# Seven products instead of eight for a third of the later gate and value projections

## The chip, the core and the metric

The kernel runs on one NeuronCore of a Trainium2 chip. The metric is the device time of one execution, in microseconds (us); a time of several runs is their median. The core has five engines that work side by side, each through its own instructions in the order in which they were written: TensorE (PE in the profile; PEld is its loading of weights), VectorE (DVE), ScalarE (ACT), GpSimd (POOL) and SyncE (SP, which here only starts transfers). Matrix products are written into PSUM, which has eight banks of 128 partitions by 512 float32.

## The reference: what is computed

Inputs are q, k, v of shape (4 batches, 8 heads, 768 tokens, 64), 16 centroids for each head, and the weights of a gated feed-forward layer, `w_gate` and `w_val` (512 x 1536) and `w_out` (1536 x 512). The part before the feed-forward layer is attention within clusters:

```
q_assign = argmax(normalised q . normalised centroids)   # k_assign the same way
scores   = (q . k) / 8, or -1e9 where q_assign != k_assign
attn     = softmax(scores) . v
x        = attn with the heads side by side: 3072 tokens x 512
```

The part that the change is about:

```
gate = 1 / (1 + exp(-(x @ w_gate)))
val  = x @ w_val
out  = (gate * val) @ w_out
```

## The kernel before

**Types and layout.** Products take float16 operands and sum in float32, except the turning of inputs (a product with an identity) and the products with centroids, which take float32. Batches are `b` = 0..3; each has two token groups, `gr` = 0 and 1. Both groups of a later batch have 384 tokens; in batch 0 they have 256 and 512. So there are eight groups. Heads go in pairs, four pairs to a batch.

**Attention.** For each group and pair of heads, PE makes scores (L986), ACT their exponentials from one of two score buffers of two banks each (`sc`, L1010), PE multiplies these with the values (L1037) into one bank (`av`), and DVE divides by the sums (L1062, L1067). The result `xn` is turned by a DMA of the SP queue (L1095), seldom by PE (L1075), into `x`, four chunks of 128 features by the group's tokens. The inputs of the next batch are brought in meanwhile: loads into `nat` buffers, DVE transposes (L573), POOL casts (L628, and L499 for the values), products with centroids (L665), a few DVE steps that make the cluster rows, and DMAs that place them.

**Feed-forward layer.** `feed` (L1359) makes the 12 feature chunks of one group. `proj` (L1365) is the product of one chunk: four PE instructions (L1372) that take the four chunks of `x` against a 128 x 128 block of weights each, with the group's tokens as columns (384 for most), into one of three `ring` banks. A chunk needs two of them, one for the gate and one for the value. ACT makes the tanh of the gate's bank into a `gt` buffer (L1390), and DVE multiplies it with the value's bank into `hT` (L1401). `project` (L1165) then makes the output rows of two blocks of 128 tokens at a time. It does so already by seven products for eight (Strassen's scheme in Winograd's form): five sums of `hT` parts on DVE (L1221), seven products of six instructions of 256 columns (L1252) in two banks, and ACT, DVE and POOL steps that add up between the products (L1277 to L1325). `sum_weights` (L1127) makes the sums of `w_out` once.

**What sets the order.** No instruction is placed by hand. `Order` (from L39) is a planner that runs when the kernel is built. Every step is a task with an engine, an assumed duration, the tasks that it depends on, a due time and the buffers that it takes or uses. `schedule` goes through time, and at each step gives the engine that is free first the task that can start first (within 0.02 us: the one that is due first). The order in which tasks are chosen is the order in which they are emitted, for each engine. A task that takes a buffer must get one of the tag's slots: `free_slots` (L70) gives the slots of a tag in turn, so a task waits for the slot whose turn it is. Tags can inherit slots of another tag (`HEIRS`): the buffers named `late` (loads of later batches, and spare room in the last `project`) are slots of `nat` that are no longer needed.

Of the kernel before, what the change touches and what calls it, by code (L numbers as in the profile page):

```python
# [9 lines left out]
FP = mybir.dt.float32  # L10
# [28 lines left out]
class Order:  # L39
# [6 lines left out]
    ANY = ()  # L46
# [154 lines left out]
def kernel(  # L201
# [32 lines left out]
        "nat": 9, "t32": 4, "even": 6, "odd": 6, "oht": 3, "t1": 2, "mx": 2, "ohf": 2,  # L234
# [13 lines left out]
        "gt": ([128, 512], FP), "out2": ([128, 2, DM], FP),  # L248
# [35 lines left out]
    NVP = 6  # L284
# [21 lines left out]
    S1, T1 = 96, 52.6  # L306

    def due_at(slot):
        return T1 + (slot - S1) * (0.414 if slot < S1 else 0.826)

    def due_ffn(work):
        return 36.0 + work * 1.82
# [93 lines left out]
    c4 = od.add("DVE", 1.65, c_scale, [c1], due=-8.8, seq=[c2])  # L406
# [85 lines left out]
    def load_v(b, p, eng, due, due_cast, early=0.0, behind=()):  # L492
# [5 lines left out]
                "POOL", 0.5,  # L498
# [58 lines left out]
    def prepare(b, grp, due, step, act=(), queues=("SP",), split=False):  # L557
# [5 lines left out]
        for p, nm in sides:  # L563
            t32[p, nm] = Buf("t32")
            for half in range(2):
                if quarters(b, p):

                    def turn_blocks(p=p, nm=nm, half=half):
# [10 lines left out]
                        "DVE", 0.55, turn_blocks, nat[b, p, nm], due, lat=0.15,  # L579
# [20 lines left out]
                def copy(p=p, nm=nm, half=half, rb_=rb_):  # L600
# [11 lines left out]
                    "ACT" if (nm, half) in act else "DVE", 0.5, copy,  # L612
                    [tr], due, lat=0.15, uses=[rb_, t32[p, nm]],
# [4 lines left out]
        for p in grp:  # L618
            ev, od_ = aug[b, p] = Buf("even"), Buf("odd")
            prev = []  # L620
            for half in (0, 1) if split else (None,):
# [13 lines left out]
                for nm in ("k", "q"):  # L635
# [3 lines left out]
                            "POOL", 0.83 * part, lambda nm=nm, cast=cast: cast(nm),  # L639
# [34 lines left out]
        for half in range(2):  # L674
# [10 lines left out]
            def back(cols=cols, oh=oh, half=half):  # L685
# [4 lines left out]
                "DVE", 0.53,  # L690
                lambda t1=t1, half=half: turn_scores(take(t1)[:n], rg.tile[:n, half, :QB]),
                [cl], due, acq=[t1], uses=[rg],
            )
            a2 = od.add(
                "DVE", 0.52,
                lambda t1=t1, mx=mx: top_scores(take(mx)[:n], t1.tile[:n]),
                [a1], due, acq=[mx], uses=[t1], lat=0.0,
            )
            a3 = od.add("DVE", 0.55, same, [a2], due, acq=[oh], uses=[t1, mx], lat=0.0)
            if quarters(b, grp[0]):  # L700
                a3 = od.add("DVE", 0.25, weigh, [a3, c_small], due, uses=[oh], lat=0.0)
            a5 = od.add(
                "DVE", 0.38, back, [a3], due, seq=turned[-1:],
# [4 lines left out]
            if split or half:  # L708
                n_ = 0
                cs = cols if split else ALL  # L710
                for e in range(2):
                    for pos, p in enumerate(grp):
                        for g, nm in ((2 * pos, "k"), (2 * pos + 1, "q")):
# [7 lines left out]
                                [a5, shifted[b, p, half]], due - (20.0 if (b, grp[0]) == (1, 0) else 0),  # L721
                                uses=[oht, aug[b, p][e]], lat=1.5,
# [5 lines left out]
    def place(b, p, ohf, tiles, last, due, alloc, c):  # L728
# [6 lines left out]
        for n_, (e, nm, h) in enumerate(rows):  # L735
            g = tiles.index((nm, h))
            m = od.add(
                "DVE", 0.395,
# [4 lines left out]
                [last, *alloc], due + 0.3 * n_ + (0.0 if n_ > 5 else 0.0), uses=[ohf, aug[b, p][e]],  # L743
# [13 lines left out]
    def prepare_pair(b, p, due, step, act=("q",), direct=False):  # L757
# [3 lines left out]
        for h in range(2):  # L761
            for nm in ("k", "q"):
# [15 lines left out]
                def copy(nm=nm, cols=cols, rg=rg):  # L778
# [12 lines left out]
                    "ACT" if nm in act else "DVE", 0.5, copy, [tr], due, lat=0.15, uses=[rg, t32[nm]]  # L791
# [4 lines left out]
        for nm, e in (("k", 0), ("q", 0), ("k", 1), ("q", 1)):  # L796
            to = od_ if e else ev

            def cast(nm=nm, e=e, to=to):
# [4 lines left out]
                "POOL", 0.83, cast, [cp[nm, 0], cp[nm, 1]], due + 0.1 * e,  # L804
# [27 lines left out]
        for dur, go, acq, uses in (  # L832
            (0.61, lambda: turn_scores(take(t1), rg.tile[:, :QB]), t1, [rg]),
            (0.55, lambda: top_scores(take(mx), t1.tile), mx, [t1]),
            (0.67, same, oh, [t1, mx]),
            (0.55, lambda: turn_matches(take(oht)[:, :QB], oh.tile), oht, [oh]),
        )[: 3 if direct else 4]:
            last = od.add("DVE", dur, go, [last], due, lat=0.0, acq=[acq], uses=uses)
# [24 lines left out]
    def prepare_first(due):  # L863
# [8 lines left out]
        for nm, h in (("k", 0), ("k", 1), ("q", 0), ("q", 1)):  # L872
# [34 lines left out]
            cp[nm, h] = od.add(on, 0.5, copy, [tr], due, lat=0.1, uses=[rg, t32[nm]])  # L907
# [30 lines left out]
        for dur, go, acq, uses in (  # L938
            (0.58, lambda: turn_scores(take(t1), rg.tile[:, :QB]), t1, [rg]),
            (  # L940
                0.55,
# [19 lines left out]
    def attend(block, at, slot):  # L961
# [13 lines left out]
        early = slot < 108.0  # L975
        t1 = []
        for i, (e, j) in enumerate(some):
            kb = aug[b, p][j % 2]

            def score(i=i, e=e, j=j, kb=kb):  # L980
# [16 lines left out]
                    due - (32.5 if early else 0.0), lat=0.25,  # L997
# [6 lines left out]
        def exponentials():  # L1004
# [16 lines left out]
            "ACT", 0.13 + 0.00078 * together * N, exponentials,  # L1021
            [*t1, c_small, c3], due, lat=0.2, acq=[es], uses=[sc],
# [8 lines left out]
        def value():  # L1031
# [15 lines left out]
            due + (-4.1 if last else 3.5) - (23.5 if early else 0.0), lat=0.25 if last else 0.0,  # L1047
# [52 lines left out]
        t4 = od.add("DVE", 0.17 + 0.02 * nq, rec, [t3], due - 18.0, lat=0.05, acq=[rr], uses=[av])  # L1100
        t5 = od.add("DVE", 0.14 + 0.15 * nq, norm, [t4], due - 18.0, lat=0.2, acq=[xn], uses=[av, rr])
        if not ((b, gr) == (0, 0) and p >= 2 or (b, p) == (0, NP - 1) or block == blocks[-1]):
# [11 lines left out]
                "DVE", 0.1 + 0.133 * nq, out_of_bank, [t6], due - 18.0, lat=0.2, seq=xd[:1],  # L1114
# [12 lines left out]
    def sum_weights(due):  # L1127
# [26 lines left out]
        for kind, dur in (("1112", 0.84), ("2122", 0.84), ("1122", 0.42)):  # L1154
# [10 lines left out]
    def project(b, one, two, final, many, end):  # L1165
# [45 lines left out]
        def add(to, place, x, y, op, behind=()):  # L1211
            tasks = []
            for n, (i0, i1) in enumerate(parts):
# [4 lines left out]
                        "DVE", 0.15 + 0.067 * (i1 - i0),  # L1218
                        first(
                            fresh,  # L1220
                            lambda i0=i0, i1=i1: nc.vector.tensor_tensor(  # L1221
# [4 lines left out]
                        due - -10.0 - (6.0 if end and not n else 0.0), lat=0.15, acq=fresh,  # L1226
# [11 lines left out]
        a6 = add([], lambda: a(1, 0), lambda: a(1, 0), lambda: a(0, 0), ALU.subtract, a22)  # L1238
        a7 = add([], lambda: a(0, 1), lambda: a(0, 1), lambda: a(1, 1), ALU.subtract, a12)
# [3 lines left out]
        def product(ring, bank, new, lo, hi, left_, right, deps, acq, uses, n0=0, runs=((0, NFC // 2),)):  # L1243
# [33 lines left out]
            "ACT", 0.4, first(fresh_hf, lambda: nc.scalar.mul(t_hf(), t_r1()[:, HM:], 0.5)), [m2], due, lat=0.2,  # L1277
# [4 lines left out]
            "DVE", 0.42,  # L1282
# [4 lines left out]
            "DVE", 0.42, lambda: stt(t_hf(), t_r2()[:, HM:], 0.5, t_df()[:, 1], ALU.mult, ALU.add),  # L1287
# [251 lines left out]
```

## Time and profile before

| | us |
|---|---|
| time, median of 3 runs | 315.88 (315.83 to 315.93) |
| the profiled execution, its own time | 315.89 |
| its span, from the first to the last instruction | 314.1 |
| PE busy | 307.8 (98%) |
| ACT busy | 221.3 (70%) |
| DVE busy | 206.0 (66%) |
| POOL busy | 93.4 (30%) |

The span is the time between the first and the last instruction on the core; 1.8 us of the execution's own time lie outside it. The granted clock of PE is 0.999 of full speed on the mean. In the timeline, a row is a run of like instructions: its start, how long until the last of them is done, engine, line of the kernel, operation, output<-inputs, shape and count; brackets give the idle time before it and what ended it. Matrix products overlap: the next starts before the one before is out of the array, so the time that one costs PE is the distance between starts, and the row's own duration is longer than that. Output shapes are partitions x columns.

### The profile page before, as it was taken

Reading aid. Unit: us, or ns where it says so; the run is one execution under the profiler, and the core shown is the slowest. Engines: PE = TensorE matmul, PEld = TensorE weight load, DVE = VectorE, ACT = ScalarE, POOL = GpSimd, SP = SyncE. Lnnn points to the kernel's source line nnn. Section 1 sums busy time; section 2 is a strip of 40 time slices with the busy share of each in tenths; the row PEclk is TensorE's granted clock in tenths of the full one; section 3 lists DMA queues with packets and bytes.
Section 4 is the critical chain, followed back from the end, with each engine's and each line's share of the span. In section 5 each row is a group of like instructions: output and inputs, shape, how many; then the busy total and the mean of one; then the engine's idle time right before and its main releaser. Section 6 shows DMA issues by size and latency. Waiting matters only on the chain.

```text
span 314.1 us, 7876 instructions
## 1 busy us (share of the span) xinstructions
PE 307.8 (98%) x3083; PEld 213.3 (68%) x3083; DVE 206.0 (66%) x480; ACT 221.3 (70%) x323; POOL 93.4 (30%) x140
## 2 busy tenths in 40 slices
PE   8999999999999999999999999999999999999995
PEld 4567888545668866567666876657766787667674
DVE  4999733899979659485335899576333753457684
ACT  4699999237999767777788857767788777632321
POOL 4998659551014224420202135430210021000000
PEclk9999999999999999999999999999999999999999
DMA  6999999957175669521574649631310012000103
GB/s 221 374 220 251 216 211 168 187 121 131 42 114 88 143 121 263 147 77 37 120 113 71 103 78 234 176 83 40 88 57 13 15 61 100 3 0 12 58 2 134
DMA packets 79957, 36.83 MB, mean 117 GB/s; under 512 B 64512, under 2 KB 74864, under 8 KB 79920
## 3 DMA queue, kind: packets, MB, share of 16 engines
q1 hardware_dynamic: 72048, 24.30, 33.1%
q0 software_dynamic: 6864, 11.01, 17.6%
q10 hardware_dynamic: 1008, 1.02, 0.9%
q8 instruction: 24, 0.39, 0.5%
q14 instruction: 13, 0.11, 0.1%
HBM read 28.34 MB, written 6.29 MB: 110 GB/s over the span
## 4 chain that ended last, share of the span: by engine, by line
PE 91%; DVE 7%; issue 1%; ACT 0%; DVEq 0%; ACTq 0%
PE ring L1372 40%; PE sc L986 18%; PE ring L1252 14%; PE av L1037 10%; PE sc L665 3%; PE sc L1252 3%; DVE even L552 2%; DVE odd L552 1%; PE av L348 1%; DVE t L527 1%; DVE ohf L541 1%; PE ring L881 1%; DVE mx L534 1%; DVE t L555 1%; PE ring L595 1%
## 5 line engine op out<-in xcount | busy, mean ns | idle before, releaser
L1010 ACT ACTIVATE es<-sc,nbias 128x768 f16<-128x768 f32 (+1 forms) x189 | 167.1, 913 | 34.6 <-PE sc L986 33.1
L1401 DVE SCALAR_TENSOR_TENSOR hT<-gt,ring 128x384 f16<-128x384 f32 (+2 forms) x96 | 53.0, 552 | 58.9 <-PE ring L1372 55.0
L1372 PE MATMUL ring<-x,wv 128*128 128x384 f16 (+2 forms) x384 | 78.1, 326 | 0.0
L1372 PE MATMUL ring<-x,wg 128*128 128x384 f16 (+2 forms) x384 | 78.1, 326 | 0.0
L1390 ACT ACTIVATE gt<-ring 128x384 f32<-128x384 f32 (+2 forms) x96 | 47.1, 490 | 35.1 <-PE ring L1372 20.9
L1037 PEld LDWEIGHTS <-es 128*128 128x128 f16 x1152 | 55.1, 97 | 17.6
L1037 PE MATMUL av<-vp,es 128*128 128x65 f16 x1152 | 60.2, 193 | 0.0
L1372 PEld LDWEIGHTS <-wv 128*128 128x128 f16 x384 | 34.7, 98 | 20.7 <-issue 0.6
L1372 PEld LDWEIGHTS <-wg 128*128 128x128 f16 x384 | 34.5, 97 | 19.6 <-issue 0.2
L628 POOL CAST even<-t 128x768 f16<-128x768 f32 x24 | 20.1, 839 | 70.2 <-DVE t L573 60.1
L1252 PEld LDWEIGHTS <-hT 128*128 128x128 f16 x294 | 27.1, 98 | 4.6 <-issue 0.6
L1304 POOL TENSOR_TENSOR diff<-out 128x256 f32<-128x256 f32 x9 | 7.5, 834 | 70.4 <-ACT out L1298 70.4
L986 PE MATMUL sc<-even 80*128 80x384 f16 (+2 forms) x120 | 26.7, 293 | 1.5 <-DVE even L552 0.7
L986 PEld LDWEIGHTS <-odd 80*128 80x128 f16 x216 | 19.9, 98 | 10.1 <-issue 2.5
L986 PE MATMUL sc<-odd,even 80*128 80x384 f16 x96 | 26.5, 326 | 0.1
L986 PEld LDWEIGHTS <-even 80*128 80x128 f16 x216 | 19.8, 98 | 9.8 <-issue 1.9
L986 PE MATMUL sc<-even,odd 80*128 80x384 f16 (+2 forms) x120 | 26.1, 293 | 0.1
L986 PE MATMUL sc<-odd 80*128 80x384 f16 x96 | 25.9, 325 | 0.0
L499 POOL CAST vp<-nat 128x384 f16<-128x384 f32 x32 | 17.0, 570 | 18.5 <-DMA nat<-in_v_dram 14.9
L573 DVE STREAM_TRANSPOSE t<-nat 128x384 f32<-128x384 f32 x40 | 20.9, 551 | 0.0
L1252 PEld LDWEIGHTS <-s 128*128 128x128 f16 x180 | 16.7, 98 | 3.3 <-DVE diff L1283 0.6
L1067 DVE TENSOR_TENSOR xn<-av,rr 128x384 f16<-128x384 f32 (+2 forms) x36 | 18.3, 509 | 0.9
(113 smaller groups left out, 315.3 us busy)
## 6 DMA issues: line engine op xcount, KB each, us to landing
out_dram<-out SPq DMA_DIRECT2D x21, 256.0 KB, 2.6
nat<-in_v_dram POOLq DMA_DIRECT2D x12, 384.0 KB, 4.5
nat<-in_k_dram SPq DMA_DIRECT2D x32, 96.0 KB, 2.9
nat<-in_q_dram SPq DMA_DIRECT2D x32, 96.0 KB, 3.0
odd<-even SPq DMA_DIRECT2D x12, 192.0 KB, 4.5
nat<-in_k_dram SPq DMA_DIRECT2D x5, 384.0 KB, 5.9
nat<-in_q_dram SPq DMA_DIRECT2D x5, 384.0 KB, 5.8
nat<-in_v_dram SPq DMA_DIRECT2D x4, 384.0 KB, 7.3
```

The source lines that it names most:

```text
L499: lambda e=e: nc.gpsimd.tensor_copy(vps[i % NVP][:, e, :, 0:D], buf.tile[:, e, :, :]),
L552: nc.vector.transpose(to.bitcast(FP), of.bitcast(FP))
L573: nc.vector.transpose(t[:, half * QB : (half + 1) * QB].rearrange("p (c x) -> p c x", x=128), blocks_[:, half],)
L628: nc.gpsimd.tensor_copy(t[:, NM[nm], cols], t32[p, nm].tile[:, cols])
L986: nc.tensor.matmul(out=to, lhsT=kb.tile[0:80, 0, e * QB + j // 2 * 128 : e * QB + (j // 2 + 1) * 128], rhs=qb_.tile[0:80, 1, e * QB + c0 * ...
L1010: i = nc.scalar.activation(to, of, AF.Exp, bias=nbias, scale=D ** -0.5 if quarters(b, p) else scale,).ins
L1037: nc.tensor.matmul(out=av.tile[:, g : g + D + 1], lhsT=es.tile[:, i * N + c * 128 : i * N + (c + 1) * 128], rhs=vp[:, e, j, :], start=firs ...
L1067: nc.vector.tensor_tensor(take(xn)[:, :nq].rearrange("p c (e d) -> p (c e) d", d=D), sums()[:, :, 0:D], rr.tile[:, : 2 * nq].unsqueeze(2). ...
L1252: nc.tensor.matmul(out=ps[:, lo:hi], lhsT=left_()[:, i], rhs=right(i)[:, n0 : n0 + w], start=new and i == 0, stop=i == NFC // 2 - 1, skip_ ...
L1372: nc.tensor.matmul(out=ps[:, :N], lhsT=ws[fc // FPG][:, dcc, fc % FPG, :], rhs=xb.tile[:, dcc, :N], start=(dcc == 0), stop=(dcc == NDC - 1),)
L1390: lambda rg=rg, gt=gt: nc.scalar.activation(take(gt)[:, :N], rg.tile[:, :N], AF.Tanh, scale=0.5),
L1401: nc.vector.scalar_tensor_tensor(t[:, fc, :N], gt.tile[:, :N], 1.0, rv.tile[:, :N], ALU.add, ALU.mult)
```

## The change

`feed` gets a second way to make two neighbouring chunks at once, `seven_products`. The chunks `fa` and `fa + 1` with `fa` in `WP` = (2, 4, 8) are made by it in the five groups (1,0), (1,1), (2,0), (2,1), (3,0), and those with `fa` in (2, 4) in group (3,1); 17 times in all. The two groups of batch 0 keep the old way throughout.

One use replaces four calls of `proj` (two gates, two values: 16 instructions of 384 columns) by seven products of four instructions of 192 columns each: 28 instructions. The gate's and the value's weights side by side are one matrix of 2 x 2 blocks (first and second half of the 512 features; gate and value), and `x` another (halves of the features; halves of the tokens). The sums of weight blocks, `wss`, are made once by DVE (`sum_up_weights`, 12 instructions of 512 columns). The sums of `x` blocks are made once for each group by DVE (`differ`, four instructions of 384 columns, into the buffer `tb`). The products go into three banks: X takes the first, sixth, seventh and fourth product on top of each other, Y the fifth and third, Z the second. Between them ACT copies X or Y out (`copied`, three times) and DVE adds a bank to what was copied (`added`, three times). Two tanh on ACT (`bent`) and two multiplications on DVE (`gated`) follow, as many as before, each for both chunks and half of the tokens. In the last group X and Y are the two banks of one `sc` buffer, where no attention is left.

Around it:

- `ANY = ("ring",)`: a task that takes a `ring` bank takes the one that is free first, in any order.
- In `project`, one of the five DVE sums, `a7`, goes to POOL, except in the last group.
- Room is made: `x` buffers 4 to 2, `gt` 3 to 2, `oht` 3 to 2, `oh` 3 to 2, `ohf` 2 to 1, value buffers (`vps`) 6 to 5; `late` gets three slots of `nat` instead of six, the others go to `pu` (two) and `tb` (one), and `p5` (two) is new.
- The planner's assumed durations, latencies and due times are set anew, so the order on every engine shifts somewhat. The numbers of all other instructions stay as they were.

The core of the diff:

```diff
-    ANY = ()
+    ANY = ("ring",)
...
-        "oh": 3, "es": 4, "rr": 3, "xn": 4, "x": 4,
-        "hT": 2, "gt": 3, "out2": 2, "s22": 1, "s11": 1, "s12": 1, "half": 1, "diff": 1,
-        "sc": 2, "av": 1, "ring": 3,
+        "oh": 2, "es": 4, "rr": 3, "xn": 4, "x": 2,
+        "hT": 2, "gt": 2, "out2": 2, "s22": 1, "s11": 1, "s12": 1, "half": 1, "diff": 1,
+        "sc": 2, "av": 1, "ring": 3, "p5": 2,
     }
-    HEIRS = {"late": ("nat", (3, 4, 5, 9, 10, 11)), "wsum": ("nat", (6, 7, 8))}
+    HEIRS = {"late": ("nat", (3, 4, 5)), "pu": ("nat", (9, 10)), "tb": ("nat", (11,)), "wsum": ("nat", (6, 7, 8))}
...
+    WP = (2, 4, 8)
+    wss = const.tile([128, len(WP), 4, 2, 2, 128], HP, name="wss")
-    NVP = 6
+    NVP = 5
...
+        for to, x, y, op in (
+            (s1, v1, v2, ALU.add), (s3, g1, v1, ALU.subtract), (s2, s1, g1, ALU.subtract), (s4, g2, s2, ALU.subtract),
+        ):
...
+        seven = WP[: {(0, 0): 0, (0, 1): 0, (1, 0): 3, (1, 1): 3, (2, 0): 3, (2, 1): 3, (3, 0): 3, (3, 1): 2}[b, gr]]
...
+                    (0, lambda: x_part(0, 1), lambda: x_part(0, 0)), (1, lambda: x_part(1, 1), lambda: t_part(0)),
+                    (2, lambda: x_part(1, 1), lambda: x_part(0, 1)), (3, lambda: x_part(1, 0), lambda: t_part(1)),
...
+        def seven_products(fa, work):
...
+                    for f in range(2):
+                        for d in range(2):
+                            nc.tensor.matmul(
+                                out=ps[:, f], lhsT=w_[:, d, f], rhs=x_()[:, d], start=new and not (f or d),
+                                stop=d == 1, skip_group_check=True,
+                            )
...
+            m1 = product(X, True, g1, lambda: x_part(0, 0), [], 0)
+            m5 = product(Y, True, s1, lambda: t_part(0), [], 0.02, 1)
+            m2 = product(Z, True, g2, lambda: x_part(1, 0), [], 0.04)
+            k1 = copied(0, X, m1)
+            k5 = copied(2, Y, m5, "ACT", 1)
+            a11 = added(0, Z, [m2, k1])
+            m6 = product(X, False, s2, lambda: t_part(1), [k1], 1)
+            m3 = product(Y, False, s4, lambda: x_part(1, 1), [k5], 1.02, 1)
+            k2 = copied(1, X, m6)
+            a12 = added(1, Y, [m3, k2], 1)
+            m7 = product(X, False, s3, lambda: t_part(2), [k2], 2)
+            a22 = added(2, X, [m7, k5])
+            m4 = product(X, False, v2, lambda: t_part(3), [a22], 3)
+            b11, b12 = bent(0, a11), bent(1, a12)
+            gated(0, lambda: bank(X), [b11, m4], [X])
+            gated(1, lambda: held(2), [b12, a22], [p5])
...
         for fc in range(NFC):
             due = due_ffn(work)
+            if fc in seven:
+                seven_products(fc, work)
+                work += 2.6 * w * 7 / 8
+                continue
+            if fc - 1 in seven:
+                continue
...
-        a7 = add([], lambda: a(0, 1), lambda: a(0, 1), lambda: a(1, 1), ALU.subtract, a12)
+        a7 = add([], lambda: a(0, 1), lambda: a(0, 1), lambda: a(1, 1), ALU.subtract, a12, "POOL")
```

More of the change, by code (lines that the diff above doesn't have):

```diff
@@ L611, in prepare @@
                 cp[p, nm, half] = od.add(
-                    "ACT" if (nm, half) in act else "DVE", 0.5, copy,
-                    [tr], due, lat=0.15, uses=[rb_, t32[p, nm]],
+                    "ACT" if (nm, half) in act else "DVE", 0.475, copy,
+                    [tr], due, lat=0.11, uses=[rb_, t32[p, nm]],
                 )
@@ L790, in prepare_pair @@
                 cp[nm, h] = od.add(
-                    "ACT" if nm in act else "DVE", 0.5, copy, [tr], due, lat=0.15, uses=[rg, t32[nm]]
+                    "ACT" if nm in act else "DVE", 0.375 if nm in act else 0.475, copy, [tr], due, lat=0.15 if nm in act else 0.11, uses=[rg, t32[nm]]
                 )
@@ L906, in prepare_first @@
             turns.append(tr)
-            cp[nm, h] = od.add(on, 0.5, copy, [tr], due, lat=0.1, uses=[rg, t32[nm]])
+            cp[nm, h] = od.add(on, 0.375, copy, [tr], due, lat=0.16, uses=[rg, t32[nm]])
             rows = [
@@ L1209, in project, with add @@
         parts = ((0, 3), (3, NFC // 2)) if end else ((0, NFC // 2),)
-        def add(to, place, x, y, op, behind=()):
+        def add(to, place, x, y, op, behind=(), on="DVE"):
             tasks = []
+            on = "DVE" if end else on
             for n, (i0, i1) in enumerate(parts):
@@ L1406, in feed @@
                 od.add(
-                    "DVE", 0.1 + 0.4 * w, gated, [g2, v1], due - 15.0, lat=0.2, seq=done[:1],
+                    "DVE", 0.06 + 0.405 * w, gated, [g2, v1], due - 14.0, lat=0.14, seq=done[:1],
                     acq=[] if fc else [hb], uses=[gt, rv] + ([hb] if fc else []),
```

224 lines of the change are left out of this document (167 added, 57 removed).

## The prediction

> **What bounds the kernel now.** I began with the page's first lines and the chain that ended last.
>
> ```profile
> span 314.1 us, 7876 instructions
> ...
> PE 307.8 (98%) x3083; PEld 213.3 (68%) x3083; DVE 206.0 (66%) x480; ACT 221.3 (70%) x323; POOL 93.4 (30%) x140
> ...
> PE 91%; DVE 7%; issue 1%; ACT 0%; DVEq 0%; ACTq 0%
> ```
>
> PE is busy in 98% of the span and makes 91% of the chain. Busy time of overlapping products can hide gaps, though, so I went to the waits of PE next, all there are:
>
> ```profile
> PE av L348 <- PEq L1523: 0.8, 1, 0.8
> PE sc L986 <- DVE even L552: 0.7, 2, 0.5
> PE sc L986 <- ACT es L1010: 0.7, 2, 0.4
> PE ring L926 <- DVE cblk L419: 0.3, 1, 0.3
> ```
>
> That is 2.5 us, and in the timeline all of it lies before 31.3 us. To see that no gap hides behind a product's tail I compared starts in the timeline of the middle (PE, then ACT):
>
> ```profile
> 151.94 0.81 PE L1372 MATMUL ring<-x,wg 128*128 128x384 f16 x4
> 152.59 0.49 PE L986 MATMUL sc<-even 80*128 80x384 f16 x2
> 152.92 0.35 PE L1037 MATMUL av<-vp,es 128*128 128x65 f16 x6
> 153.10 0.81 PE L1372 MATMUL ring<-x,wv 128*128 128x384 f16 x4
> 153.75 0.33 PE L986 MATMUL sc<-even 80*128 80x384 f16 x1
> 153.92 0.32 PE L986 MATMUL sc<-even,odd 80*128 80x384 f16 x1
> 154.08 0.35 PE L1037 MATMUL av<-vp,es 128*128 128x65 f16 x6
> ...
> 151.96 0.90 ACT L1010 ACTIVATE es<-sc,nbias 128x768 f16<-128x768 f32 x1
> 152.79 0.49 ACT L1390 ACTIVATE gt<-ring 128x384 f32<-128x384 f32 x1
> 153.18 0.90 ACT L1010 ACTIVATE es<-sc,nbias 128x768 f16<-128x768 f32 x1
> 154.28 0.90 ACT L1010 ACTIVATE es<-sc,nbias 128x768 f16<-128x768 f32 x1 [0.21 <-PE sc L986]
> ```
>
> Four 384-column products take 0.65 us from start to start (151.94 to 152.59, 153.10 to 153.75), so 0.1625 each; two scores 0.33, the same pace; six value products 0.18. Every row starts where the pace of the one before puts it. From about 38 us to the last products PE is full: a stage of 270 us in which only less PE work, or a new wait, changes the time.
>
> **The change: PE.** The order of the changed kernel has 272 products of 384 columns fewer and 476 of 192 columns more; all other PE counts are equal, so the change does what it says. No row has 192 columns. The nearest are 384 (0.1625) and 128:
>
> ```profile
> 46.77 0.33 PE L986 MATMUL sc<-even 80*128 80x128 f16 x3
> 46.95 0.33 PE L986 MATMUL sc<-even,odd 80*128 80x128 f16 x3
> 47.11 0.35 PE L1037 MATMUL av<-vp,es 128*128 128x65 f16 x6
> ```
>
> Six take 0.34 us, 0.0567 each. On the line between the two widths 192 columns cost 0.083 us. The bounds are the two rates per column: 0.0813 and 0.085. The 204 more weight loads hide: the value products load new weights every 0.030 us. Removed: 272 x 0.1625 = 44.2. Added: 476 x 0.083 = 39.5. Gain **4.7 us** (3.7 to 5.5).
>
> The Trainium skill, "TensorE: Matmul & The Clock Gate", section "Back-to-back issue gap", speaks against this: in a stream of load and product it gives 81 ns at 128 columns and 131 at 512, so narrow products are dear. An estimate by its line between these puts 28 narrow products at 2.50 us against 1.83 for 16 wide ones, 0.67 lost in each use, and the sum would be 11.4 us worse than before. The trace has 57 ns and 162 ns instead, so I keep the rows.
>
> **ScalarE and VectorE.** ACT gets 51 copies of a 384-column bank (17 uses x 3; the tanh number stays). The nearest row is the tanh of the same size: 0.39 us to the next start (152.79 to 153.18), 0.49 to its end. That is 51 x 0.39 = 20 us, ACT 221 to 241, 78% of the new span. DVE gets 51 additions (nearest L1401, one bank and one SBUF input, 552 ns: 28), 24 differences (L1221 at 384 columns, 351 ns: 8.4) and 12 weight sums (L1148 and L1151, 485 and 425 ns: 5.5), and loses ten `a7` (L1221, 0.55: 5.5): 206 to 242, 78%. POOL gets the ten: its nearest row, L1304, takes 834 ns for 256 columns, so 2.5 us for 768 (at least the 0.84 of a cast of that size): 25 us, 93 to 118. The weight sums come when `t` has been copied; there DVE has gaps of 0.7 to 2.2 us between 37 and 54 us. No engine but PE becomes the bound on the mean, so these 20 and 36 us cost nothing while PE has something to do; they cost where PE waits for one of them.
>
> **The new waits.** Products into X wait for a copy or an addition: m1, copy, m6, copy, m7, addition, m4. What stands behind a waiting product on PE is everything, scores too. One hand-over needs: the end of the product's pace to ACT's start 0.20 (154.08 to 154.28), the copy 0.49, and PE's start 0.05 (in the chain of waits, an exponential ends at 31.18 and PE starts at 31.23): 0.74; through DVE 0.20 + 0.55 + 0.05 = 0.80. The order has other PE work in between. With the paces above, the 15 uses in `ring` banks have 1.02 to 1.67 us between m1 and m6, 0.98 to 1.81 between m6 and m7, 1.02 to 1.66 between m5 and m3, 1.01 and more between m7 and m4, about 1.35 on the mean. A free engine is always in time. If an exponential (0.83 from start to start) has just begun on ACT, 1.57 is needed. Exponentials run half the time (167 of 314). At a cover of 1.35, what is late is the case that more than 0.61 of the 0.83 is left: 0.5 x 0.22 / 0.83 = 13%, 0.11 on the mean. At the shortest covers, spare 0.28: 33%, 0.28 on the mean. For 45 hand-overs through ACT that is 0.6 us at the mean cover and 4.1 if all were short. I take **1.2**, since a third of them are below 1.2 us.
>
> Edits with one answer: fewer `x`, `gt`, `vps` buffers, the three-slot `late`, `ANY` and the new durations change the order only. PE never waits for a bank, load or `x` after 31 us now, so free banks in any order save nothing alone; they find X, Y and Z a place, since X stays taken for some 5 us. At the start DVE paces the work until 30 us; the order puts four copies ahead of the second pair's rows there, instructions equal. I take 0, within 0.7 either way.
>
> **Sum.** 315.89 (the profiled execution, equal to the median of 315.88 for this purpose; 1.8 of it outside the span) - 4.7 + 1.2 = **312.4**.
>
> **Rivals.**
> *Hand-overs eat the gain.* If covers act like the shortest, 4.1 instead of 1.2: 315.3; with the low gain of 3.7, 316.3. About 315.8, no change. For it: ACT was already full in some stretches (19.2 of 20 us at 80 to 100). Against: PE lost nothing there.
>
> *Slower: VectorE stands behind GpSimd's long sum.* The trace has such a stop (DVE, POOL, PE):
>
> ```profile
> 97.92 1.19 DVE L1221 TENSOR_TENSOR hT<-hT 128x768 f16<-128x768 f16 x1
> ...
> 97.87 0.83 POOL L628 CAST even<-t 128x768 f16<-128x768 f32 x1 [1.95 <-PE av L1037]
> ...
> 97.94 0.82 PE L1252 MATMUL ring<-nat,hT 128*128 128x256 f16 x6
> 98.59 0.49 PE L986 MATMUL sc<-odd 80*128 80x384 f16 x2
> ```
>
> A sum that takes 0.52 alone took 1.19, until POOL's cast was done; PE went on (0.65 to the next start). The changed order has a two-input DVE sum within two instructions of the moved `a7` in six of the ten places, and L1283 behind it in most, for which m5 waits. A stop of 2.5 less some 0.7 of other PE work less 0.5 that DVE has to spare is 1.3, six times 7.8: 315.89 - 4.7 + 1.2 + 7.8 = 320.2. It turns the sign from 0.6 us a place. The Trainium skill, "SBUF — State Buffer", section "Who interferes with whom", says that a VectorE instruction with two SBUF inputs and a GpSimd one that reads SBUF exclude each other for the whole instruction; by that rule the new `gated` with `p5` and the differences are hit too; the trace agrees where both ran (1.19 for 0.52).
>
> *A load comes late.* With three `late` slots a load waits for the slot, and SP's transfers behind it. One exposed load (four starts of 0.65 and 2.9 to landing, 5.5) gives 317.9. Against: PE never waits for a transfer now.
>
> *Narrow products are dear.* If 192 columns took what 256 do (97.94 to 98.59 for six, 0.108), 476 x 0.108 = 51.4: 324.3. Against: the 128-column rows.
>
> **Chances.** Forecast 0.75, its own range 310.2 (gain 5.5, no waits, with 0.2 less at the start) to 314.8 (gain 3.7, waits 2.0, start 0.6); no change 0.09; GpSimd 0.09; late load 0.06; dear products 0.01. A change under 0.2% (0.6 us) is about what a measurement of this kernel can't tell from none. Faster 0.75, same 0.09, slower 0.16. The range reaches over the no-change case to 316.8 and leaves out most of the last three: 310.2 to 316.8.
>
> **What would show it.** Right: narrow products 0.083 apart; PE waits after 38 us of 1 to 2 us in all, on copies or additions; ACT and DVE near 241 and 242 busy. Wrong: rows `sc` or `ring` on PE waiting for DVE L1286 or `p5` beside a POOL sum; a PE wait on `nat`, `x` or `vp`; 192-column rows more than 0.085 apart; a first stretch over 38 us.

## The result and the profile after

The changed kernel takes **324.11 us** (median; 323.32 to 326.47) against 315.80 for the kernel before in the same comparison: ratio 1.0276, 95% interval 1.0238 to 1.0314. It is slower, by 8.3 us. The forecast was 312.4, the range 310.2 to 316.8. The profiled execution took 323.68 us, and with it the table below comes to 7.8 us; two of the six executions had a mean granted clock of 0.994 and 0.995 and took 326.47 and 325.73, while the other four, at 0.999 or 1.0, took 323.32 to 324.53.

First the page of the changed kernel: span, busy time, and the chain that ended last.

```profile
span 321.9 us, 8392 instructions
...
PE 305.7 (95%) x3287; PEld 225.2 (70%) x3287; DVE 241.7 (75%) x556; ACT 237.7 (74%) x374; POOL 110.1 (34%) x150
...
PE 60%; DVE 16%; DMA 12%; ACT 5%; issue 3%; POOL 2%; SPq 1%; DVEq 0%; ACTq 0%; POOLq 0%
```

The side engines are as busy as forecast (ACT 237.7 for 241, DVE 241.7 for 242). PE's share of the chain, though, fell from 91% to 60%: DVE and DMA are on it now. So PE waits; these are the waits of PE that matter here, with what they name (total us, times, longest):

```profile
PE ring L1255 <- DVE diff L1286: 3.1, 2, 2.2
PE sc L1255 <- DVE nat L1224: 1.5, 1, 1.5
PE sc L988 <- ACT es L1012: 1.2, 4, 0.6
PE ring L1402 <- DVE hT L1576: 1.0, 2, 0.7
...
PE sc L1478 <- DVE nat L1509: 0.4, 1, 0.4
PE sc L1478 <- ACT p L1497: 0.3, 1, 0.3
```

Only the last two lines are hand-overs of the seven products (L1478). The larger ones are products of other steps: the out projection (L1255) behind VectorE's combinations and sums, the scores (L988) behind late exponentials, the plain projections (L1402) behind a late gate.

These waits leave out what hides under the tail of a product, so I also added up PE by starts: each product gets its pace (0.1625 us for 384 columns, 0.0825 for 192, and so on, as the prediction did for its rows), and what a start is later than that is a gap. All terms are from the two profiled executions:

| | before | after | difference |
|---|---|---|---|
| products at their pace | 299.3 | 294.4 | -4.9 |
| gaps up to 38 us | 8.55 | 8.88 | +0.3 |
| gaps after 38 us | 1.75 | 13.57 | +11.8 |
| from the last product's start to the end | 3.72 | 4.30 | +0.6 |
| span (with 0.77 before the first product) | 314.1 | 321.9 | +7.8 |

The products gained what they should. The loss is 11.8 us of new gaps after 38 us. The gaps over 0.4 us are at 71.37 (0.85), 73.58 (0.49), 80.34 (0.59), 186.28 (2.39), 220.31 (0.51), 225.63 (0.95), 252.92 (1.09), 291.00 (1.70), 296.70 (0.45) and 301.31 (0.54). They fall into three kinds.

**Kind 1, 71 to 81 us.** The kernel has no narrow products there yet. The stretch from 60 to 80 us in the windows by engine, before and then after (columns: PE, PEld, DVE, ACT, POOL busy, each with its instructions):

```profile
60.00:80.00 20.00, 20.00 (x137) 9.63 (x136) 19.03 (x40) 10.63 (x16) 7.06 (x11) 1.00 0.65 134
```

```profile
60.00:80.00 20.00, 18.90 (x97) 8.10 (x96) 19.59 (x38) 6.62 (x12) 12.70 (x19) 1.00 0.45 129
```

PE has 40 instructions fewer, ACT 4 us less, POOL 5.6 us more. The timeline of POOL shows why: the last loads of the next batch's `q`, before and then after (start, us):

```profile
46.83 2.28 POOL L323 DMA_DIRECT2D nat<-in_q_dram  x3 [1.33 <-DMA nat<-in_v_dram]
51.09 2.64 POOL L323 DMA_DIRECT2D nat<-in_q_dram  x3
```

```profile
63.89 3.10 POOL L325 DMA_DIRECT2D nat<-in_q_dram  x4 [2.58 <-DVE t L575]
```

They start 13 us later, after POOL stood 2.58 us until VectorE's transposes (L575) had emptied a slot. What follows from them (casts, centroid products, matches) moves into this stretch: the sixteen centroid products that started at 70.6 start at 76.3. No wait of PE after 38 us names a load. Part of the way from the late loads to PE can be followed at 71.37, in the timeline of POOL, VectorE and PE:

```profile
68.62 1.14 POOL L630 CAST even<-t 128x768 f16<-128x768 f32 x1
```

```profile
69.00 1.15 DVE L1149 TENSOR_TENSOR nat<-wo 128x512 f16<-128x512 f16 x1
```

```profile
71.37 1.02 PE L1402 MATMUL ring<-x,wg 128*128 128x512 f16 x4 [0.69 <-DVE hT L1576]
```

A cast of POOL and a sum of `w_out` weights on VectorE fall together, and the sum takes 1.15 us instead of 0.42; the gate L1576 stands behind it, and PE behind the gate. Another such sum takes 0.95 (71.53), ahead of the gap at 73.58.

**Kind 2, beside the moved `a7`.** VectorE, POOL and PE in the timeline around 186 us:

```profile
183.11 1.99 DVE L1224 TENSOR_TENSOR hT<-hT 128x768 f16<-128x768 f16 x1
...
185.81 0.42 DVE L1286 SCALAR_TENSOR_TENSOR diff<-ring,half 128x256 f32<-128x256 f32 x1
```

```profile
183.00 1.69 POOL L1224 TENSOR_TENSOR hT<-hT 128x768 f16<-128x768 f16 x1 [1.23 <-DVE s L1224]
```

```profile
186.28 0.81 PE L1255 MATMUL ring<-wo,s 128*128 128x256 f16 x6 [2.22 <-DVE diff L1286]
```

VectorE's sum takes 0.55 alone; here it ends 0.41 us after POOL's. The combination L1286 stands behind it with one instruction in between, and PE behind that: a gap of 2.39. The same is at 252.92, and at 291.00, where PE waits for the next sum; the three gaps make 5.2 us. In four other places VectorE began first and POOL was the one that took longer (1.88 or 1.89 for 1.64); no gap of PE follows there. Behind the last of these four a difference (L1440, at 254.99) took 1.79 us instead of 0.34, until 0.21 after POOL's sum ended. So the differences are hit by this as well, as the prediction said of the slower case, here without a gap of PE.

**Kind 3, the rest**: 220 to 226, and the last group's own hand-overs at 296.70 and 301.31.

### The profile page after: what moved, and what is told of

Same layout as the page of the kernel before. It is cut to its first block, busy times and chain, and to the rows that moved or that the text cites. A ratio compares the mean times of both kernels' runs of the same rounds, so it can differ in the third digit from the quotient of the medians.

```text
span 321.9 us, 8392 instructions
## 1 busy us (share of the span) xinstructions
PE 305.7 (95%) x3287; PEld 225.2 (70%) x3287; DVE 241.7 (75%) x556; ACT 237.7 (74%) x374; POOL 110.1 (34%) x150
## 4 chain that ended last, share of the span: by engine, by line
PE 60%; DVE 16%; DMA 12%; ACT 5%; issue 3%; POOL 2%; SPq 1%; DVEq 0%; ACTq 0%; POOLq 0%
PE sc L988 14%; PE ring L1255 13%; PE ring L1402 13%; PE ring L1478 8%; PE av L1039 7%; DMA nat<-in_q_dram 4%; DMA wo<-in_moe_w_out_dram 4%; DMA nat<-in_k_dram 3%; DVE hT L1576 2%; PE sc L1255 2%; ACT es L1012 2%; DVE hT L1224 2%; DVE t L575 1%; PE sc L667 1%; ACT nat L1497 1%
## 5 line engine op out<-in xcount | busy, mean ns | idle before, releaser
L1039 PEld LDWEIGHTS <-es 128*128 128x128 f16 x1152 | 53.4, 97 | 11.8 <-DVE xn L1069 0.2
L1565 ACT ACTIVATE gt<-ring 128x384 f32<-128x384 f32 (+2 forms) x62 | 31.0, 501 | 28.5 <-PE ring L1402 25.4
L1402 PE MATMUL ring<-x,wg 128*128 128x384 f16 (+2 forms) x248 | 50.4, 325 | 1.1 <-DVE hT L1576 1.0
L1402 PE MATMUL ring<-x,wv 128*128 128x384 f16 (+2 forms) x248 | 50.4, 326 | 0.0
L1576 DVE SCALAR_TENSOR_TENSOR hT<-gt,ring 128x384 f16<-128x384 f32 (+2 forms) x62 | 33.9, 547 | 16.5 <-PE ring L1402 15.0
L1402 PEld LDWEIGHTS <-wg 128*128 128x128 f16 x248 | 23.4, 97 | 16.6 <-issue 2.6
L1402 PEld LDWEIGHTS <-wv 128*128 128x128 f16 x248 | 23.0, 97 | 13.6
L1255 PEld LDWEIGHTS <-hT 128*128 128x128 f16 x294 | 27.5, 98 | 5.6 <-DVE hT L1224 1.0
L1224 POOL TENSOR_TENSOR hT<-hT 128x768 f16<-128x768 f16 x8 | 13.9, 1736 | 46.5 <-DVE nat L1224 23.9
L988 PE MATMUL sc<-even 80*128 80x384 f16 (+2 forms) x120 | 26.5, 293 | 1.5 <-DVE t L529 0.8
L988 PE MATMUL sc<-odd,even 80*128 80x384 f16 x96 | 26.0, 326 | 0.2 <-ACT es L1012 0.2
L988 PE MATMUL sc<-odd 80*128 80x384 f16 x96 | 26.0, 325 | 0.1
L988 PE MATMUL sc<-even,odd 80*128 80x384 f16 (+2 forms) x120 | 25.4, 293 | 0.6 <-ACT es L1012 0.6
L1509 DVE TENSOR_TENSOR nat<-ring,nat 128x384 f32<-128x384 f32 x32 | 17.2, 551 | 11.0 <-ACT nat L1497 6.2
L1478 PEld LDWEIGHTS <-wss 128*128 128x128 f16 x272 | 22.8, 97 | 3.4 <-issue 1.0
L988 PEld LDWEIGHTS <-odd 80*128 80x128 f16 x216 | 18.9, 98 | 8.4 <-issue 4.9
L988 PEld LDWEIGHTS <-even 80*128 80x128 f16 x216 | 19.5, 98 | 7.0 <-issue 2.3
L575 DVE STREAM_TRANSPOSE t<-nat 128x384 f32<-128x384 f32 x40 | 21.6, 557 | 2.9 <-DMA nat<-in_q_dram 2.4
L1255 PEld LDWEIGHTS <-s 128*128 128x128 f16 x180 | 16.8, 97 | 7.1 <-issue 3.5
```

The costliest lines, as they stand in the source:

```text
L575: nc.vector.transpose(t[:, half * QB : (half + 1) * QB].rearrange("p (c x) -> p c x", x=128), blocks_[:, half],)
L988: nc.tensor.matmul(out=to, lhsT=kb.tile[0:80, 0, e * QB + j // 2 * 128 : e * QB + (j // 2 + 1) * 128], rhs=qb_.tile[0:80, 1, e * QB + c0 * ...
L1039: nc.tensor.matmul(out=av.tile[:, g : g + D + 1], lhsT=es.tile[:, i * N + c * 128 : i * N + (c + 1) * 128], rhs=vp[:, e, j, :], start=firs ...
L1224: lambda i0=i0, i1=i1: Q2[on].tensor_tensor(place()[:, i0:i1], x()[:, i0:i1], y()[:, i0:i1], op),
L1255: nc.tensor.matmul(out=ps[:, lo:hi], lhsT=left_()[:, i], rhs=right(i)[:, n0 : n0 + w], start=new and i == 0, stop=i == NFC // 2 - 1, skip_ ...
L1402: nc.tensor.matmul(out=ps[:, :N], lhsT=ws[fc // FPG][:, dcc, fc % FPG, :], rhs=xb.tile[:, dcc, :N], start=(dcc == 0), stop=(dcc == NDC - 1),)
```

## The experiments

The theories: **T1**, VectorE stands behind GpSimd's long sum (the rival on record as the slower case); **T2**, or **T4** in the later runs, the seven products' copies, additions and differences delay other work; **T3**, the smaller buffers or the planner's new numbers. Every time below is a median, with the ratio to the kernel before and its 95% interval.

### Taking the change apart

e1, a7 back on VectorE:

```diff
-a7 = add([], ..., ALU.subtract, a12, "POOL")
+a7 = add([], ..., ALU.subtract, a12, "DVE")
```

> The change with the ten sums a7 back on VectorE, all else of it kept. In the trace of the changed kernel PE stands 5.9 us in all where a sum of VectorE with two SBUF inputs lay beside one of them (186.28: 2.39; 218 to 221: 0.73; 252.92: 1.09; 291.00: 1.70). Theory 1 (VectorE stands behind GpSimd's long sum): 324.1 - 5.9 = 318.2, give or take 1.5, and no VectorE sum of 768 columns over 1.3 us. Theory 2 (the hand-overs of the seven products and the sums for them fill VectorE): the ten sums come on top, 324 to 326. Theory 3 (the smaller buffers and the new times): within 1 of 324.

Measured 322.06 (1.0204; 1.0177 to 1.0230). The move of a7 costs 2.05 us, a third of what T1 expected. Of the three gaps beside a7, 0.63 (186.95), 0.11 (259.07) and 0.25 (289.05) are left, which is 4.2 less; new ones take about half of it back: 0.48 at 128.56 and 148.97, 0.39 at 184.81, 0.38 at 161.04. Two of these four name VectorE, which has ten sums more here, and two name late exponentials. By the two intervals the 2.05 may be off by some 1.5 us.

e2, the kernel before with this one move:

```diff
-"DVE", 0.15 + 0.067 * (i1 - i0),
+"DVE" if end else on, ... if end or on == "DVE" else 1.7,
...
-a7 = add([], ..., a12)
+a7 = add([], ..., a12, "POOL")
```

> The kernel before with only this taken from the change: ten of the sums a7 go to GpSimd, with 1.7 us as the planner's duration. Theory 1: each place where a VectorE sum with two SBUF inputs lies beside one costs PE 1 to 2 us; with three to six such places 319 to 322. Theories 2 and 3: VectorE has less to do and PE waits for nothing, 315.5 to 316.5.

Measured 316.96 (1.0049; 1.0029 to 1.0069): 1.2 us up, between the two expectations. The mechanism is there without the rest of the change, at a lower price: one place stops PE for 0.70 us, at 286.35, where VectorE's sum took 1.81 beside POOL's 1.64.

e3, no seven products at all, a7 on VectorE:

```diff
-seven = WP[: {(0, 0): 0, (0, 1): 0, (1, 0): 3, ... (3, 1): 2}[b, gr]]
-if not wsums_of: ... sum_up_weights(...)
+seven = ()
```

> The change without the seven products (all eight groups by eight) and with a7 on VectorE: what is left of it is the smaller buffers, free banks in any order, and the planner's new durations and times. Theory 1: 315.5 to 317, since PE never waited for those. Theory 3: 320 or more, and the stops of PE at 71 to 81 us (1.9 us in the changed kernel) are still there.

Measured 318.36 (1.0076; 1.0059 to 1.0093). With no work added and none removed, 2.6 us are lost. That lies between the two expectations; T3 has a part. The gaps at 71.42 (0.74), 73.47 (0.32) and 80.22 (0.58) are there, and POOL issues its last `q` loads as late as in the changed kernel.

e4, as e3, but a7 left on GpSimd:

```diff
+seven = ()
 a7 = add([], ..., ALU.subtract, a12, "POOL")
```

> The change without the seven products, a7 left on GpSimd. Theory 1: 3 to 6 us over the run that has a7 on VectorE and no seven products, with VectorE sums of 768 columns at 1.5 to 2 us. Theory 2: the same time as that run within 1 us, since without the seven products VectorE has room.

Measured 320.73 (1.0166; 1.0145 to 1.0186): 2.4 over e3, again between the two. The runs are steps from one kernel to the other: 2.6 (e3 over before), 3.7 (e1 over e3: the seven products, although they take 4.9 from PE), 2.05 (changed kernel over e1: a7). Steps of this kind add up to the whole whatever the parts do to each other, so their sum shows nothing. Only the third was also taken alone: a7 costs 2.05 with the seven products, 2.4 without them, and 1.2 in the kernel before, so its price depends on what is around it. The rest of the study asks what is in the first two.

### Buffers or numbers, copies or differences

e5, the kernel before with the change's buffer counts only:

```diff
-"oht": 3, "ohf": 2, "oh": 3, "x": 4, "gt": 3   NVP = 6
-"late": ("nat", (3, 4, 5, 9, 10, 11))
+"oht": 2, "ohf": 1, "oh": 2, "x": 2, "gt": 2   NVP = 5
+"late": ("nat", (3, 4, 5))
```

> The kernel before with only the change's buffer counts (x, gt, oht, oh, ohf, late and vp as in the change, no seven products, no new durations or times). The change without the seven products and with a7 on VectorE took 318.4, 2.6 us over before; its PE stops 1.9 us at 59 to 81 us, 1 us at 37 to 42, 0.5 at the start. Theory 3a (the smaller buffers cost it): 317.5 to 319. Theory 3b (the new durations and due times cost it): within 0.5 of 315.8.

e6, the other half: e3 with the old buffer counts.

```diff
-"oht": 2, "ohf": 1, "oh": 2, "x": 2, "gt": 2   NVP = 5
-"late": ("nat", (3, 4, 5))
+"oht": 3, "ohf": 2, "oh": 3, "x": 4, "gt": 3   NVP = 6
+"late": ("nat", (3, 4, 5, 9, 10, 11))
```

> The other half: the change's planner numbers (durations, due times, load times, free ring banks in any order) with the buffer counts of before, no seven products, a7 on VectorE. Theory 3a: within 0.7 of 315.8. Theory 3b: 317.5 to 319, with the stops at 71 to 81 us still there.

Measured 320.65 for e5 (1.0156; 1.0130 to 1.0182) and 316.20 for e6 (1.0019; 1.0008 to 1.0030). The buffers cost 4.9 us with the old numbers and 2.2 with the new (318.36 - 316.20); the new numbers soften them and are worth nothing alone. T3a holds in kind; its range, 317.5 to 319, was too low for e5.

e7 leaves the copies and additions out, e8 the differences:

```diff
-k1 = copied(0, X, m1); k5 = copied(2, Y, m5, "ACT", 1)
-a11 = added(0, Z, [m2, k1]) ... a22 = added(2, X, [m7, k5])
+k1, k5, a11, k2, a12, a22 = m1, m5, m2, m6, m3, m7
```

```diff
-if seven: (the four differences of the group)
-m5 = product(Y, True, s1, lambda: t_part(0), ...)
+m5 = product(Y, True, s1, lambda: x_part(0, 1), ...)
```

> The run with the seven products and a7 on VectorE (322.1), with the 51 copies and the 51 additions left out: the products follow each other into their banks without a hand-over, the tanh reads the banks, the differences and the weight sums stay. The output is then not the reference's. Theory 4a (copies on ScalarE and additions on VectorE delay what stands behind them): 322.1 less 2 to 4, so 318 to 320, and the rows with exponentials late behind copies are gone; stops at 184 to 226 us, where the differences meet the sums of the out projection, stay. Theory 4b (the differences do it all): within 1 of 322.

> The same run with the 24 differences left out instead (the narrow products read x itself, so the output is not the reference's); copies and additions stay. Theory 4a: within 1 of 322, since the stops behind copies stay. Theory 4b: 322.1 less 2 to 4, 318 to 320, with the stops at 184.8, 186.9, 219.1 and 226.1 us gone.

Measured 318.24 for e7 (1.0076; 1.0047 to 1.0106) and 319.98 for e8 (1.0133; 1.0116 to 1.0151), from 322.06. Without copies and additions the kernel is 3.8 faster, without differences 2.1: neither theory alone, but both parts. Counted by starts, PE's gaps after 38 us fall from 11.2 (e1) to 7.9 and 9.2, and those between 60 and 80 us hardly change (1.4, 1.4 and 1.2), so it is not the loads that moved. 1.1 of the 3.8 are the last group's own hand-overs, which e7 leaves out too; the rest lies elsewhere. The gaps did not go where the theories said: those at 219 and 226 us are gone in e7, where the differences stay, and one near 219 is still there in e8 (0.87). So 3.8 and 2.1 are what these kernels gain, in an order that shifts too. Together they are 5.9 of the 8.6 us (3.7 lost and 4.9 not gained) that the seven products cost in waits; the other 2.7, the twelve weight sums among them, were not separated.

How a copy delays other work is seen in e1 at 128 us, in the timeline of ACT and of PE:

```profile
127.56 0.94 ACT L1012 ACTIVATE es<-sc,nbias 128x768 f16<-128x768 f32 x1
128.35 0.53 ACT L1497 COPY p<-ring 128x384 f32<-128x384 f32 x1
```

```profile
127.75 0.49 PE L1478 MATMUL ring<-nat,wv 128*128 128x192 f16 x4
128.56 0.48 PE L988 MATMUL sc<-odd 80*128 80x384 f16 x2 [0.32 <-ACT es L1012]
```

Just ahead of this exponential ACT had a copy and two tanh of 384 columns (126.37 to 127.72). The narrow products ran without a gap; the scores behind them waited for the bank that the late exponential reads, a gap of 0.48.

### Which buffer, and how much a reshuffle moves

All from e3; e9 gives back `late` and `vp`, e10 `x` and `gt`, e11 the match tiles. e12 is the kernel before with only `ANY = ("ring",)`, a reshuffle of the order with no change of work.

```diff
e9:  "late": ("nat", (3, 4, 5, 9, 10, 11)), NVP = 6
e10: "x": 4, "gt": 3
e11: "oht": 3, "ohf": 2, "oh": 3
e12: ANY = ("ring",)
```

> The run without the seven products and with a7 on VectorE (318.4; the same new numbers with all buffers of before 316.2), with only the six late slots and the six vp tiles given back. If the load slots carry the 2.2 us between those two (the rival that a load comes late): 316.2 to 316.8. If x, gt or the match tiles do: 317.8 to 319.

> The same run with only the four x and the three gt tiles given back. The stops at 59, 71, 73 and 80 us name ring banks that wait for the tanh and the gate. If x and gt carry it: 316.2 to 316.8, and the stops of 0.74 and 0.32 us at 71 to 74 us shrink to those of the run with the old buffers (0.09 and 0.27). If not: 317.8 to 319.

> The same run with only the match tiles given back (oht 3, oh 3, ohf 2). The stop of 0.58 us at 80 us names VectorE's transposes of the match scores (L529). If the match tiles carry it: 316.2 to 316.8 and no such stop. If not: 317.8 to 319.

> The kernel before with only free ring banks taken in any order. It removes no work and adds none; it reshuffles the order on PE and VectorE. Theory: within 0.7 of 315.8. It also shows how much a mere reshuffle moves the time, so what size of difference between the other runs can be read as a cause.

Measured: e9 **315.38** (0.9984; 0.9972 to 0.9996), e10 318.13 (1.0072; 1.0050 to 1.0093), e11 322.02 (1.0195; 1.0154 to 1.0235), e12 315.87 (1.0005; 0.9988 to 1.0022). The load slots or `vp` carry all of it, `x` and `gt` nothing. e11 missed on the other side: more room for matches made it 3.7 us worse. Its gaps are at 36.99 (1.94, PE waiting for a `q` load), 74.35 (1.60) and 83.93 (1.38), so my reading is that the three slots are still its trouble, in an order that meets the late loads worse; no run with these tiles and six slots was made, so this is not shown. e12 says that one reshuffle of a kernel with its loads on time moves it by 0.1 us. For kernels with three slots e11 is the measure: there a step that adds no work moved it by 3.7. The parts found between such kernels (3.7, 2.05, 3.8, 2.1) rest on their gaps, therefore, and not on the times alone.

### The slots alone; fewer uses with more slots

e13 is e3 with only the six slots back. e14, e15 and e16 have the seven products again, with a7 on VectorE, and trade uses for slots; all three have one `pu` and one `p5` buffer, where the change has two of each:

```diff
e13: "late": ("nat", (3, 4, 5, 9, 10, 11)), NVP = 5, seven = ()
e14: WP = (4,),      6 slots, p5 1, pu and tb tiles of their own, NVP = 6
e15: WP = (4, 8),    5 slots, p5 1, pu a tile of its own, tb in nat 11, NVP = 6
e16: WP = (2, 4, 8), 4 slots, p5 1, pu in nat 10, tb in nat 11, NVP = 6
```

> The change without the seven products, a7 on VectorE (318.4), with only the six late slots given back, the vp tiles left at five. If the load slots alone carry the 3.0 us that late and vp together gave back: 315.2 to 316. If the sixth vp tile carries it: 318 or more.

> The change with a7 on VectorE and six late slots, and the seven products in one place of each of the last six groups (6 uses instead of 17), their tiles in memory of their own. Theory A (each use costs more in work that waits behind its copies, additions and differences than its 0.29 us of PE: 322.06 - 318.36 = 3.7 us for 17 uses, 0.22 each): 315.4 + 1.3 = 316.7. Theory B (the uses gain as soon as the loads are on time): 315.4 - 6 x 0.29 = 313.7.

> The same with two places in each of the six groups (12 uses) and five late slots. Theory A: 315.4 + 2.6 = 318.0. Theory B: 315.4 - 12 x 0.29 = 311.9. If five slots are too few, PE stops at 60 to 81 us again.

> The same with the change's 17 uses and four late slots. Theory A: 315.4 + 3.7 = 319.1, and up to 1 more if four slots are too few. Theory B: 315.4 - 4.9 = 310.5.

Measured: e13 **315.41** (0.9989; 0.9979 to 0.9999), e14 316.85 (1.0036; 1.0023 to 1.0049), e15 317.46 (1.0051; 1.0036 to 1.0066), e16 324.51 (1.0277; 1.0253 to 1.0301).

e13 settles the first part: three slots instead of six for the next batch's loads cost 2.95 us (318.36 - 315.41). POOL in e13 issues its last `q` loads, and the windows show the stretch, thus:

```profile
49.45 0.74 POOL L325 DMA_DIRECT2D nat<-in_q_dram  x1 [0.56 <-DMA nat<-in_k_dram]
50.97 0.74 POOL L325 DMA_DIRECT2D nat<-in_q_dram  x1 [0.78 <-DMA nat<-in_q_dram]
```

```profile
60.00:80.00 20.00, 20.00 (x110) 8.96 (x109) 19.80 (x43) 8.27 (x13) 7.88 (x11) 1.00 0.55 124
```

The loads are out by 51.7 us, POOL is back at 7.9 us of busy time, and PE at 20.00 of 20.

With the loads on time six uses cost 1.44 us and twelve 2.05: theory A's 1.3 and 2.6, not theory B's gain. e16 missed by 5.4. Its gaps between 60 and 80 us are 4.78, more than with three slots, but its `q` loads are out by 50.7 us, as early as in e13. The largest, 3.0 at 75.83, names a gate, and this is what stood ahead of the gate, on VectorE and POOL:

```profile
69.27 3.11 DVE L1149 TENSOR_TENSOR nat<-wo 128x512 f16<-128x512 f16 x1
```

```profile
70.70 2.94 POOL L501 CAST vp<-nat 128x384 f16<-128x384 f32 x6
```

A sum of weights that takes 0.42 alone took 3.11 beside POOL's casts, nine of them in a row from 69.03, and the next one 1.51. It is the stop of kind 2, with casts in the place of a7. Nearly all of the other 1.8 us is in slow products: from 76.5 to 79.9 us the granted clock was half of full speed, and products of 512 columns started 0.43 apart instead of 0.22. No other profile shows such a drop between 10 us and its last product, not even the changed kernel's behind its gap of 2.39; why it came here was not tested. e16 has hand-over gaps in `ring` banks as well (1.20 at 129.98), with its single `pu` and `p5`. It tells nothing about four slots, then, and how much of the price of the uses in e14 and e15 comes from the single buffers was not separated.

### The uses away from the worst places

In e14 the gaps stood in few places: 0.80 in the last group's hand-overs, 1.32 at 183.6 and 0.22 at 174.3, where VectorE had alternated four differences with five sums of the out projection. e17 and e18 leave the last group by eight and put the differences behind the sums:

```diff
-seven = WP[: n if b else 0]
+seven = WP[: n if b and (b, gr) != (B - 1, 1) else 0]
-"DVE", 0.28, differ, ..., due_ffn(work) - 6.5, ...
+"DVE", 0.28, differ, ..., due_ffn(work) + 4.0, ...
```

> The run with one place in each group (316.85), with the last group left by eight (5 uses) and the differences put behind the sums of the out projection in the planner's order. In that run PE stopped 0.80 us in the last group's use, 1.32 at 183.6 and 0.22 at 174.3, and the tail after the last products was 0.9 us longer. Theory A, refined (a use costs what waits behind its copies, additions and differences; away from the last group and from the sums little waits): 315.4 - 5 x 0.29 + 0.5 to 1.0 of stops = 314.5 to 315.0. If every use costs 0.22 wherever it is: 316.5.

> The run with two places and five late slots (317.46), with the last group by eight (10 uses) and the differences behind the sums. Its stops outside the last group were 3.7 us, 1.45 of them beside the differences. Refined theory A: 315.4 - 10 x 0.29 + 2.3 to 3.7 = 314.8 to 316.2. If every use costs 0.22 wherever it is: 317.6.

Measured 316.02 for e17 (1.0008; 0.9995 to 1.0020), between its two expectations, and 315.91 for e18 (1.0006; 0.9993 to 1.0019), within theory A's. With both steps together the uses are no longer dear, but they gain nothing either: 5 uses are 0.6 over e13, 10 uses 0.5. Which of the two steps helped was not separated. In e17 the differences now stand behind the sums, and one gap remains:

```profile
181.85 0.68 DVE L1328 SCALAR_TENSOR_TENSOR out<-ring,diff 128x512 f32<-128x512 f32 x1
182.45 0.34 DVE L1440 TENSOR_TENSOR tb<-x,tb 128x384 f16<-128x384 f16 x1
182.72 0.34 DVE L1440 TENSOR_TENSOR tb<-x 128x384 f16<-128x384 f16 x1
182.99 0.41 DVE L1286 SCALAR_TENSOR_TENSOR diff<-ring,half 128x256 f32<-128x256 f32 x1
```

```profile
183.45 0.82 PE L1255 MATMUL ring<-wo,s 128*128 128x256 f16 x6 [0.90 <-DVE diff L1286]
```

PE's gap there is 1.06, for a combination (L1286) that had two differences and another combination (L1328) right ahead of it. Five uses save 1.45 us of products, this gap and one of 0.22 take 1.28 back: the last product starts at 309.83 us in e17 and at 309.91 in e13. The rest of e17's 0.6 is in its tail (4.5 us from that start to the end, 3.8 in e13); what lengthens the tail was not settled. In e18 the gaps after 38 us are 3.6 more than in e13, against 2.9 saved; the largest is the same one (1.29 at 183.89).

The fastest kernels are e9 and e13, 0.4 us under the kernel before: by their intervals a little faster, but within the 0.2% that I called not to be told from no change. They have none of the seven products.

## Why the prediction was wrong

**The products: right.** 4.7 us forecast, 4.9 found; 192-column products start 0.0825 apart, 0.083 taken. The rival of dear narrow products is out.

**The hand-overs: right in size by luck.** 1.2 us forecast, for the 45 copies of the fifteen uses in `ring` banks. These show no gap over 0.06. The gaps at hand-overs in the changed kernel are 0.45, 0.12 and 0.54, all in the last group, whose X and Y share a `sc` tile and which has no scores in between; the forecast had nothing for its two uses. And I took the hand-overs for the only new waits.

**"Edits with one answer ... change the order only": the first step that failed.** It was costed at 0 and measured 2.6 (e3), by e13 the three late slots. I had a rival with 317.9, and this part alone gives 318.36, but the nearness is luck: the rival was one load that PE waits for and that is out of the way after 5.5 us. In the changed kernel no wait of PE after 38 us names a load. What comes late is the work behind the loads, which meets VectorE's sums and gates. What misled me was the argument against it, "PE never waits for a transfer now". That is a row of a kernel with six slots. It says that six are enough, and nothing of three.

**"These 20 and 36 us cost nothing while PE has something to do": the second step that failed.** It put 1.2 us of waits in the place of 8.6. I worked out whether PE waits for the new instructions, and not what stands behind them in the queues of ACT and DVE: exponentials behind copies and tanh, sums and combinations of the out projection behind differences. At 75% busy on the mean an engine still has stretches without room, and VectorE's fall at the meeting of a projection and an out projection, where the change put four differences. Taking them out gave 2.1 us, and taking out the copies and additions 3.8, 1.1 of it hand-overs.

**VectorE behind GpSimd: the mechanism right, the size off.** The rival had 7.8 us (six places at 1.3); the move of a7 costs 2.05. GpSimd's sum takes 1.64 us, not the 2.5 taken, and three places of ten stopped PE, not six. The Trainium skill, "SBUF — State Buffer", section "Who interferes with whom", says that such instructions exclude each other; the trace agrees, with 1.99, 1.75 and 2.01 on VectorE where GpSimd was first, and 1.88 to 1.89 on GpSimd where VectorE was. The price depends on who is second, and on whether PE waits for that one.

**The start**: 0 taken, 0.3 found.

**The chances.** I treated the rivals as cases of which at most one would come, and gave the two slower ones 0.15 together. The GpSimd stop and the slot loss came together, beside a third cost that I had not named, the work behind copies and differences.

## What to carry to other kernels

That nothing waits for a resource now says only that there is enough of it now: before a change takes slots from loads, follow the loads themselves, from the slot's last reader to the issue, with the new number of slots. When new work goes to engines that are not the bound, price it by what stands behind it in their queues where they are already full, not by their mean load or by the wait for the new work itself. And several small losses may all come true at once; the slow side of a range has to hold them together.

## What was not expected of the hardware

A GpSimd sum of two 128x768 f16 tiles takes 1.64 us, that is 2.1 ns a column, where its 256-column f32 row before (834 ns) gives 3.3; VectorE does the same in 0.55. When VectorE's sum began just behind GpSimd's, it was drawn out by nearly the whole of it: 2.01 (288.19), where it began 0.04 us after GpSimd's 1.64. Casts do the same: a VectorE sum of 0.42 took 3.11 beside a row of them (e16, 69.27).
